# ScalarE's queue takes only the four loads of k of block 0; all loads of v of block 0 go to SyncE's queue

## The chip, the cores and the metric

The kernel runs on one core of one Trainium2 chip. The metric is the time of one execution on the device in microseconds (us). Times are medians over several executions. Each execution also has a mean granted TensorE clock, 1.00 being full speed. The clock record of a trace begins only at 5.06 in before; before that the page prints 1.00 though nothing was recorded.

Engine names in the profile: PE is TensorE (matmuls), PEld its weight loads, DVE is VectorE, ACT is ScalarE, POOL is GpSimd, SP is SyncE. ACTq and SPq are what the ScalarE and SyncE sequencers do themselves, here mostly issuing transfers (DMA).

## The reference

Attention inside chunks of 64 tokens, and then a bilinear feed-forward network (FFN) on its output:

```python
# q, k, v: (8, 8, 576, 64) float32; chunk = 64
scores = (q_c @ k_c.T) / 8;  attn = softmax(scores);  out = attn @ v_c
x = out.transpose(0, 2, 1, 3).reshape(4608, 512)
a = x @ w_a;  b = x @ w_b                  # 512 x 1536 each
return (a * b) @ w_out                     # 1536 x 512
```

## The kernel before

Tokens are worked on in nine blocks of 512. For block 0, q, k and v are loaded in small pieces, so that the first matmuls can start early; v comes in two halves (`hu`), each in four loads of 128 KB. Weights follow on SyncE's queue, first two half-width pairs, then full pairs. Two feature tiles of 128 share a pair; POOL casts each to bf16, and PE works with the cast.

```python
def load_half_v(hu, gs, eng):                       # L147
    for g in gs:
        eng.dma_start(
            out=f32[hu][2][:, g * 256:(g + 1) * 256].rearrange("p (h d) -> p h d", h=4),
            in_=v[0, 4 * hu:4 * hu + 4, g * 128:(g + 1) * 128, :].transpose([1, 0, 2]),
        )
# ... the start of the program; the order of statements is the order on each engine
for m in range(4):
    load_quads(m, 0, q, nc.sync)                    # L140
    load_quads(m, 1, k, nc.scalar)
# ... table load on ScalarE
load_half_v(0, (0, 1), nc.sync)
load_half_v(1, range(4), nc.sync)
# ...
queue_half(0, 0); queue_half(0, 1)                  # weights of pair 0: w_b, w_a, w_b, w_a (L154)
queue_w(1); queue_w(2)                              # pairs 1 and 2, w_b and w_a each

fill(2)                                             # filler matmuls that keep PE busy (L539)
quad_cast(0, 0, V)
quad_turn(0, 0, A)                                  # PE transposes q, ScalarE evacuates (L167)
load_half_v(0, (2, 3), nc.scalar)                   # <-- on ScalarE, in program order HERE
quad_cast(0, 1, V); quad_turn(0, 1, V); fill(1, n=128); quad_cast(1, 1, V)
# ... casts on POOL
quad_scores(0); expo(0, 0)                          # score products (L340), exponential on ScalarE (L245)
quad_turn(1, 0, V); quad_turn(1, 1, V); quad_turn(2, 0, A)
quad_scores(1); expo(0, 1)
# ... sums, logarithm, inverse, values of both halves; a filler; then the FFN of block 0 (L398)
```

In the trace of before the landings of transfers are counted on eight semaphores. The first eight loads wait for none of them; each of the next eighteen, on SyncE as on ScalarE, waits on one of the eight and is issued after the load last counted there has landed: the ninth, SyncE's first v load, at 4.35 us after a k load that landed at 4.33, and ScalarE's two v loads at 8.23 and 9.39 after loads that landed at 8.21 and 9.37. And later units of attention get their transposed q and k by a transpose transfer, also on SyncE's queue (L216), whose result the score products of that unit (L234) wait for.

```python
turn_unit(7); load_unit(8, (1, 2)); load_unit(9, (0,))
cast_unit(7, (2,)); some_sums(24); cast_unit(8, (0, 1))
for tg in range(4):
    step(); outs(1, (tg,))                          # four output stores, on SyncE's queue (L438)
    if tg == 0: slot(5, None)
cast_unit(8)
turn_unit(8)                                        # behind these stores in SyncE's queue (L216)
load_unit(9)
```

The softmax here doesn't subtract the row's maximum and nothing guards it: scores larger than these inputs give would overflow.

Of the kernel before, what the change touches and what calls it, by code (L numbers as in the profile page):

```python
# [11 lines left out]
def kernel(  # L12
# [10 lines left out]
    nc = tc.nc  # L23
# [118 lines left out]
            in_=src[0, 2 * m:2 * m + 2, 0:BLK, :].rearrange("h (p r) d -> p h (r d)", r=4),  # L142
        )

    def load_half_v(hu, gs, eng):
        for g in gs:
            eng.dma_start(  # L147
                out=f32[hu][2][:, g * 256:(g + 1) * 256].rearrange("p (h d) -> p h d", h=4),
                in_=v[0, 4 * hu:4 * hu + 4, g * 128:(g + 1) * 128, :].transpose([1, 0, 2]),
            )  # L150
# [152 lines left out]
    def quad_cast(m, x, eng):  # L303
        c = (m % 2) * 512
        copy(
            eng,
            qkb[m // 2][:, x, c:c + 512].rearrange("p (r h d) -> p h r d", r=4, h=2),
            f32[m // 2][x][:, c:c + 512].rearrange("p (h r d) -> p h r d", h=2, r=4),
        )

    def quad_turn(m, x, eng):

        t = nextF().bitcast(BF16)
        c0 = (m % 2) * 512
        for r in range(4):
            c = r * 128
            nc.tensor.transpose(
                t[:, c:c + 128], qkb[m // 2][:, x, c0 + c:c0 + c + 128], identity
            )
        n = 8 * x + 4 * (m % 2)  # L320
        dst = qkT[m // 2][:, n:n + 4, :]
        if x == 0:
            copy(eng, dst, t[:, 0:512].rearrange("p (r t) -> p r t", r=4))
        else:
            copy(
                eng,
                dst.rearrange("p a b -> p (a b)").rearrange("p (t r) -> p t r", r=4),
                t[:, 0:512].rearrange("p (r t) -> p t r", r=4),
            )
# [220 lines left out]
    with tc.manual_schedule():  # L550
# [6 lines left out]
        for m in range(4):  # L557
# [5 lines left out]
                name=nc.get_next_instruction_name(), act_func_set_id=6, ins=[], outs=[]  # L563
            )
        )
        load_half_v(0, (0, 1), nc.sync)
        load_half_v(1, range(4), nc.sync)

        def queue_half(i, h):
            for n, src in (("b", moe_w_b), ("a", moe_w_a)):  # L570
# [28 lines left out]
        fill(2)  # L599
        quad_cast(0, 0, V)  # L600
        quad_turn(0, 0, A)
        load_half_v(0, (2, 3), nc.scalar)
        quad_cast(0, 1, V)
        quad_turn(0, 1, V)
        fill(1, n=128)
# [288 lines left out]
```

## Time and profile before

| | before |
|---|---|
| time, 3 runs | 317.68 us median (316.77 to 318.01) |
| the profiled run | 316.13 us, span 314.3 us, mean granted clock 0.989 |
| first exponential starts | 9.87 us |
| second score products start | 10.51 us |
| first FFN matmul starts | 19.12 us |

Lines of the profile's page of the kernel before: busy time of the engines, granted clock in 40 equal slices of the span (in tenths), and shares of the chain of work that ended last.

```profile
span 314.3 us, 7288 instructions
...
PE 304.6 (97%) x2902; PEld 177.3 (56%) x2902; DVE 186.6 (59%) x371; ACT 133.9 (43%) x227; POOL 123.8 (39%) x159
...
PEclk9789999999999999999999999999999999999999
...
PE 93%; DMA 3%; ACT 2%; POOL 0%; issue 0%; DVE 0%; POOLq 0%; DVEq 0%; ACTq 0%; SPq 0%
```

PE is the limit almost everywhere; only the first slices differ. The chain before, in order of time (start, duration, what), has its transfers at the very start:

```profile
0.73 3.60 DMA f<-in_k_dram
...
4.76 4.61 DMA f<-in_v_dram
...
9.39 0.43 ACTq L147
...
9.87 0.60 ACT E L245
...
10.51 0.44 PE PS L340 x16
```

The first exponential comes after a v load and after ScalarE's issue of another one, though it needs no v. The timeline of before, ScalarE and then PE, shows it (start, duration, engine, line, operation; in brackets the idle time before it and what ended it):

```profile
5.47 0.59 ACT L167 COPY qkT<-F 128x512 bf16<-128x512 bf16 x1 [1.36 <-PE F L317]
8.23 1.59 ACTq L147 DMA_DIRECT2D f<-in_v_dram  x2
9.87 0.60 ACT L245 ACTIVATE E<-PS 128x512 bf16<-128x512 f32 x1 [3.81 <-DMA f<-in_v_dram]
...
6.44 0.42 PE L340 MATMUL PS<-qkT 64*64 64x64 bf16 x16 [0.51 <-DVE qkT L169]
...
10.51 0.42 PE L340 MATMUL PS<-qkT 64*64 64x64 bf16 x16 [2.68 <-ACT E L245]
```

The first score products are ready at 6.86 us, but ScalarE is held by its two v loads, and PE then stands until 10.51. Stretches of five microseconds of before (columns: length, busy time of PE, PEld, DVE, ACT and POOL with instruction counts, granted clock, busy share of the DMA engines, GB/s) show what follows for the clock:

```profile
5.00:10.00 5.00, 2.31 (x39) 1.75 (x38) 2.71 (x5) 0.72 (x2) 2.97 (x5) 1.00 1.16 342
10.00:15.00 5.00, 3.56 (x96) 2.64 (x96) 1.72 (x3) 4.38 (x8) 1.96 (x6) 0.69 1.18 327
15.00:20.00 5.00, 4.73 (x53) 2.03 (x45) 2.58 (x4) 2.65 (x5) 3.62 (x8) 0.63 1.09 382
20.00:25.00 5.00, 5.00 (x25) 2.29 (x24) 1.81 (x3) 1.76 (x3) 4.24 (x8) 1.00 1.09 385
```

From 11.9 to 18.7 us PE has half its clock, and the transfers run at 327 to 385 GB/s.

### The profile page before, as it was taken

Reading aid. Unit: us, or ns where it says so; the run is one execution under the profiler, and the core shown is the slowest. Engines: PE = TensorE matmul, PEld = TensorE weight load, DVE = VectorE, ACT = ScalarE, POOL = GpSimd, SP = SyncE. Lnnn points to the kernel's source line nnn. Section 1 sums busy time; section 2 is a strip of 40 time slices with the busy share of each in tenths; the row PEclk is TensorE's granted clock in tenths of the full one; section 3 lists DMA queues with packets and bytes.
Section 4 is the critical chain, followed back from the end, with each engine's and each line's share of the span. In section 5 each row is a group of like instructions: output and inputs, shape, how many; then the busy total and the mean of one; then the engine's idle time right before and its main releaser. Section 6 shows DMA issues by size and latency. Waiting matters only on the chain.

```text
span 314.3 us, 7288 instructions
## 1 busy us (share of the span) xinstructions
PE 304.6 (97%) x2902; PEld 177.3 (56%) x2902; DVE 186.6 (59%) x371; ACT 133.9 (43%) x227; POOL 123.8 (39%) x159
## 2 busy tenths in 40 slices
PE   7599999999999999999999999999999999999995
PEld 3344455874444476447644765477446744674474
DVE  3443444543447764967496749574967476646663
ACT  2643317646335542653265326442644164413320
POOL 2578869876264037402630164016500400040023
PEclk9789999999999999999999999999999999999999
DMA  7999999999999999999399249943700300020003
GB/s 262 322 383 393 380 267 244 222 272 224 204 198 254 183 219 267 185 279 208 136 257 214 68 113 216 245 100 133 136 2 0 117 22 0 3 102 31 2 0 135
DMA packets 145842, 55.00 MB, mean 175 GB/s; under 512 B 126224, under 2 KB 139792, under 8 KB 145808
## 3 DMA queue, kind: packets, MB, share of 16 engines
q1 hardware_dynamic: 143664, 53.23, 69.7%
q10 hardware_dynamic: 2144, 1.31, 1.3%
q8 instruction: 22, 0.36, 0.5%
q14 instruction: 12, 0.10, 0.1%
HBM read 37.75 MB, written 9.44 MB: 150 GB/s over the span
## 4 chain that ended last, share of the span: by engine, by line
PE 93%; DMA 3%; ACT 2%; POOL 0%; issue 0%; DVE 0%; POOLq 0%; DVEq 0%; ACTq 0%; SPq 0%
PE F L398 60%; PE F L479 19%; PE F L420 6%; PE F L251 2%; PE PS L234 2%; DMA f<-in_v_dram 1%; PE PA L267 1%; DMA f<-in_k_dram 1%; PE F L539 1%; ACT E L245 1%; PE PS L340 1%; POOL part L497 0%; ACT lns L277 0%; ACT inv L281 0%; ACT qkT L167 0%
## 5 line engine op out<-in xcount | busy, mean ns | idle before, releaser
L398 PE MATMUL F<-xT,wb 128*128 128x512 bf16 (+1 forms) x460 | 112.6, 366 | 0.0
L398 PE MATMUL F<-xT,wa 128*128 128x512 bf16 (+1 forms) x460 | 112.4, 366 | 0.0
L409 ACT CAST bsb<-F 128x512 bf16<-128x512 f32 (+1 forms) x115 | 64.1, 558 | 105.9 <-PE F L398 105.6
L410 DVE TENSOR_TENSOR ab<-F,bsb 128x512 bf16<-128x512 f32 (+1 forms) x115 | 75.2, 656 | 51.8 <-PE F L398 45.6
L398 PEld LDWEIGHTS <-wa 128*128 128x128 bf16 x460 | 45.0, 98 | 48.4
L398 PEld LDWEIGHTS <-wb 128*128 128x128 bf16 x460 | 43.6, 98 | 44.1
L497 POOL TENSOR_TENSOR part<-part 128x256 f32<-128x256 f32 x14 | 10.1, 725 | 130.0 <-ACT part L523 129.0
L169 POOL CAST qkb<-f 128x1024 bf16<-128x1024 f32 (+1 forms) x35 | 34.8, 1007 | 30.2 <-DMA f<-in_k_dram 17.4
L479 PEld LDWEIGHTS <-wst 128*128 128x128 bf16 x420 | 41.1, 98 | 4.8
L479 PE MATMUL F<-wst 128*128 128x256 bf16 x252 | 33.3, 273 | 0.0
L286 DVE TENSOR_TENSOR xT<-PA,inv 128x512 bf16<-128x512 f32 x32 | 21.8, 684 | 15.8 <-ACT inv L281 15.8
L497 DVE TENSOR_TENSOR osb<-F,part 128x256 f32<-128x256 f32 x56 | 22.3, 420 | 11.0 <-POOL part L497 8.7
L497 POOL TENSOR_TENSOR part<-part,osb 128x256 f32<-128x256 f32 x28 | 19.8, 727 | 11.4 <-DVE osb L497 11.3
L169 POOL CAST vb<-f 128x1024 bf16<-128x1024 f32 (+2 forms) x22 | 19.9, 914 | 10.1 <-DMA f<-in_v_dram 8.9
L479 PE MATMUL F<-wst,ab 128*128 128x256 bf16 x168 | 22.8, 273 | 0.0
L277 ACT ACTIVATE lns<-F 128x512 f32<-128x512 f32 x32 | 17.4, 594 | 10.7 <-PE F L251 10.7
L420 PE MATMUL F<-wo,ab 128*128 128x512 bf16 x96 | 21.9, 379 | 0.0
L467 DVE TENSOR_TENSOR wst<-ab 128x512 bf16<-128x512 bf16 x42 | 21.7, 518 | 0.0
L245 ACT ACTIVATE E<-PS 128x1024 bf16<-128x1024 f32 (+1 forms) x20 | 18.8, 941 | 6.4 <-DMA f<-in_v_dram 3.8
L468 DVE TENSOR_TENSOR wst<-ab 128x512 bf16<-128x512 bf16 x42 | 20.9, 497 | 0.0
L479 PE MATMUL F<-wo,wst 128*128 128x256 bf16 x168 | 20.6, 273 | 0.0
L497 DVE TENSOR_TENSOR part<-F,part 128x256 f32<-128x256 f32 x15 | 6.4, 425 | 21.3 <-POOL part L497 21.3
(52 smaller groups left out, 199.2 us busy)
## 6 DMA issues: line engine op xcount, KB each, us to landing
out_dram<-osb SPq DMA_DIRECT2D x31, 256.0 KB, 2.0
f<-in_q_dram SPq DMA_DIRECT2D x28, 256.0 KB, 4.2
f<-in_v_dram SPq DMA_DIRECT2D x28, 256.0 KB, 4.3
f<-in_k_dram SPq DMA_DIRECT2D x24, 256.0 KB, 4.0
wst<-in_moe_w_out_dram SPq DMA_DIRECT2D x6, 512.0 KB, 8.1
wst<-in_moe_w_b_dram SPq DMA_DIRECT2D x5, 512.0 KB, 7.7
wst<-in_moe_w_a_dram SPq DMA_DIRECT2D x5, 512.0 KB, 8.1
f<-in_v_dram SPq DMA_DIRECT2D x14, 128.0 KB, 3.3
```

The costliest lines, as they stand in the source:

```text
L169: eng.tensor_copy(out=out, in_=in_)
L245: nc.scalar.activation(out=e[:, :, s], in_=PS[:, :, s], func=AF.Exp, scale=scale)
L277: nc.scalar.activation(out=lns[:, cl, :], in_=SU[cl], func=AF.Ln)
L286: nc.vector.tensor_tensor(out=x.rearrange("p m (g c t) -> p c g m t", g=2, c=2)[:, cl], in0=PA[:, cl, :].rearrange(shape, g=2, m=4), in1=i ...
L398: nc.tensor.matmul(bank[:, 0:n], w[ft // 2][ft % 2][:, kt, :], x[:, kt, us[0] * 256:us[0] * 256 + n], start=(kt == 0), stop=(kt == NKT - 1),)
L409: nc.scalar.copy(out=bT[:, 0:n], in_=banks[0][:, 0:n])
L410: nc.vector.tensor_tensor(out=ab[ft][:, us[0] * 256:us[0] * 256 + n], in0=banks[1][:, 0:n], in1=bT[:, 0:n], op=MULT)
L420: nc.tensor.matmul(o, ab[ft][:, tg * 128:(tg + 1) * 128], wo[ft // 2][:, ft % 2, :], start=(ft == 0), stop=(ft == NFT - 1),)
L467: nc.vector.tensor_tensor(out=y[:, 0:2], in0=a[:, 0:2], in1=a[:, 2:4], op=ADD)
L468: nc.vector.tensor_tensor(out=y[:, 2:4], in0=a[:, 1:3], in1=a[:, 0:4:3], op=SUB)
L479: nc.tensor.matmul(o, a(i)[:, c:c + 128], b(i), start=(i == 0), stop=(i == NP - 1))
L497: eng.tensor_tensor(out=out, in0=in0, in1=in1, op=op)
```

## The change

The intent: ScalarE should not be held by v loads in front of its first exponential. All eight v loads of block 0 go to SyncE, ahead of the weights.

```diff
-    def load_half_v(hu, gs, eng):
-        for g in gs:
+    def load_half_v(hu, eng):
+        for g in range(4):
...
-        load_half_v(0, (0, 1), nc.sync)
-        load_half_v(1, range(4), nc.sync)
+        for hu in range(2):
+            load_half_v(hu, nc.sync)
...
         quad_turn(0, 0, A)
-        load_half_v(0, (2, 3), nc.scalar)
         quad_cast(0, 1, V)
```

The order of instructions differs only in this: ScalarE loses two issues, and SyncE gains two in front of its weight loads, between the first two v loads and the four of the other half.

## The prediction

> **What bounds the kernel now.** PE is busy 304.6 us of a 314.3 us span (97%); the chain of waits that ended last is 93% PE. In time order it is PE, with some ACT and DVE pieces, from 10.5 us on. Only its head is bound by transfers: k of block 0 until 4.33 us, the second v load (SyncE, 4.76 to 9.37), ScalarE's own issue of a v load (9.39 to 9.82), then the first exponential (9.87). So the change can move the first 20 us only.
>
> **What that head costs.** In the timeline the first score products end at 6.86 us. ScalarE then stands idle 3.81 us in front of its exponential, ended by a v transfer: its program order has two v loads there, each held until an earlier load lands (issued 8.23 and 9.39). PE waits 2.68 us for that exponential before the second score products (10.51), whose operand was ready at 8.25, when VectorE had turned k of the second pair.
>
> **What the change does.** It takes the two issues out of ScalarE's stream (1.59 us in its queue, plus the wait ahead). The exponential can start near 6.9. The next limit is VectorE's turn at 8.25, so the second score products move from 10.51 to about 8.4: 2.1 us. Carrying the later links on with traced durations (exponential 0.60, logarithm 1.02, inverse pair 1.15, turns 0.5 to 0.7), the first FFN matmul (19.12) comes about 2.1 us earlier. V lands before it is needed, so POOL no longer stands 3.04 us before its v casts (13.15).
>
> **A second effect, less sure.** By stretches, the granted clock is 1.00 until 11.9 us, 0.50 until about 18.7, then 1.00: after PE's hole from 7.83 to 10.51. [...] With the hole gone, PE probably keeps its clock. The long filler there took 2.0 us at 0.5; at full clock about 1.0, so about 1 us more. I give 60% to that.
>
> **What it adds.** Two more issues on SyncE before the weights, about 0.5 us each: the first weight load issues at about 10.0 instead of 8.95. I expect weights to land at nearly the same time, because the DMA engines are saturated there (busy share 1.1 to 1.28, 286 to 385 GB/s) and the same bytes pass. Weight casts finish at least 3.4 us before their matmuls (third feature tile: 20.0 against 23.44). Later transfers (turned unit 4 used at 64.1) have an estimated 2 to 4 us, which caps the gain near 3 us.
>
> **Sum.** 2.1 us if the clock still drops, about 3.1 if not; weighted 2.6. All of it is on the critical path: PE runs without gaps afterwards and the rest just shifts. Predicted **315.0 us**, 8 in 10 between **313.7 and 316.6**. Chances: faster by over 2% 0.02, within 2% 0.97, slower by over 2% 0.01.
>
> **What would show it right.** First exponential near 7 us, no v transfer ahead of it; PE's wait before the second score products under 0.7 us; first FFN matmul at 16 to 17 us; granted clock 1.00 through 12 to 18 us (or 0.5, with FFN at 17); first weight issue near 10 us, no PE wait on weight casts; then the same durations, chain still PE.
>
> **What would make it wrong.** Weights over 1 us later, so that POOL's casts hold the first FFN tiles; the half-clock stretch only moving, over the FFN start; a later transfer or turn with less slack, which gives the gain back before 80 us; the exponential held by something other than the v loads.

The sum: 2.1 us if the clock still drops, about 3.1 us if not, weighted 2.6. That PE keeps its clock without the hole, and the 60% on the last 1 us, are the author's estimate, from the order of events in the trace of before alone: a hole from 7.83 to 10.51 us, then half clock from 11.89 to 18.72.

## The result, and the profile after

| | before | after |
|---|---|---|
| time, 4 runs each | 317.6 us median (316.77 to 318.01) | 315.55 us median (315.03 to 315.74) |
| span of the profiled run | 314.3 us | 313.9 us |
| first exponential | 9.87 us | 7.32 us |
| second score products | 10.51 us | 8.71 us |
| first FFN matmul | 19.12 us | 16.12 us |
| first weight load issued | 8.95 us | 10.70 us |

The ratio is 0.9936 (95% interval 0.9912 to 0.996). Ratios are the mean time of one kernel's runs over that of the other's of the same rounds, so not quite the ratio of the medians quoted.

Already this table holds a riddle: the FFN starts 3.0 us earlier, the medians differ by 2.05 us, and the two profiled spans by only 0.4 us. (One part of it: the profiled run of before, 316.13 us at a clock of 0.989, is 1.5 us faster than the median of the four timed runs.) The page after:

```profile
span 313.9 us, 7288 instructions
...
PE 303.9 (97%) x2902; PEld 176.1 (56%) x2902; DVE 185.1 (59%) x371; ACT 133.8 (43%) x227; POOL 124.2 (40%) x159
...
PEclk9999999999999999999999999999999999999999
...
PE 66%; DMA 18%; SPq 8%; POOL 3%; ACT 1%; issue 1%; DVE 1%; ACTq 0%; POOLq 0%; DVEq 0%
```

The clock no longer drops in the head. But the chain, which was 93% PE, is now 66% PE and 26% transfers and SyncE's issues. The timeline after, ScalarE and PE, for the lines shown of before:

```profile
7.32 0.60 ACT L245 ACTIVATE E<-PS 128x512 bf16<-128x512 f32 x1 [1.03 <-PE PS L340]
...
6.85 0.42 PE L340 MATMUL PS<-qkT 64*64 64x64 bf16 x16 [0.51 <-DVE qkT L169]
...
8.71 0.42 PE L340 MATMUL PS<-qkT 64*64 64x64 bf16 x16
```

The exponential now waits for PE, as it should. The same stretches after, and one short stretch:

```profile
5.00:10.00 5.00, 3.94 (x67) 2.87 (x65) 2.93 (x6) 2.36 (x4) 2.45 (x4) 1.00 1.14 333
10.00:15.00 5.00, 3.28 (x90) 1.66 (x86) 2.64 (x5) 4.09 (x7) 2.57 (x6) 1.00 0.85 209
15.00:20.00 5.00, 4.73 (x48) 1.94 (x38) 1.99 (x3) 2.46 (x5) 2.69 (x6) 1.00 0.99 276
20.00:25.00 5.00, 3.91 (x18) 1.65 (x19) 1.39 (x3) 1.17 (x2) 3.67 (x7) 1.00 1.08 382
...
14.00:15.00 1.00, 1.00 (x14) 0.20 (x13) 0.04 (x1) 0.97 (x2) 0.19 (x1) 1.00 0.15 37
```

Now the transfers are the ones that starve: 209 GB/s instead of 327 from 10 to 15 us, and 37 GB/s in the microsecond from 14. The timeline of SyncE's queue after shows why, and PE's what it costs:

```profile
10.70 0.51 SPq L154 DMA_DIRECT2D wst<-in_moe_w_b_dram  x1
...
11.79 2.27 SPq L154 DMA_DIRECT2D wst<-in_moe_w_b_dram  x1
14.11 0.51 SPq L154 DMA_DIRECT2D wst<-in_moe_w_a_dram  x1
...
20.66 1.04 PE L398 MATMUL F<-xT,wb 128*128 128x512 bf16 x4 [0.69 <-POOL wb L169]
22.13 1.04 PE L398 MATMUL F<-xT,wa 128*128 128x512 bf16 x4 [0.43 <-POOL wa L169]
```

From 9.6 us SyncE issues one transfer per 0.55 us; the weights stand behind eight v loads, and one issue takes 2.27 us. The two causes are of different size: in slices of one microsecond the DMA engines are still busy at 0.97 to 1.12 from 10 to 14 us (227 to 283 GB/s), and fall to 0.15 only after the long issue. At the third feature tile PE waits for POOL's casts of late weights.

The timeline gives the start of the same PE work in each trace. Below, the lead over before (us; positive is earlier) at six points, the first three in the FFN of block 0 (its products with `w_a`) and the score products of units 2, 7 and 8. "After 2" and "after 3" are two more runs of the changed kernel from the experiments.

| trace (end of span) | tile 0 | tile 2 | tile 4 | unit 2 | unit 7 | unit 8 | end |
|---|---|---|---|---|---|---|---|
| before (314.32), start of the work | 19.56 | 23.44 | 26.89 | 48.60 | 98.44 | 108.09 | 314.32 |
| after (313.91), lead | 2.79 | 1.31 | 1.30 | 0.72 | 0.73 | 0.35 | 0.41 |
| after 2 (313.77), lead | 3.59 | 1.74 | 1.73 | 1.55 | 1.27 | 0.92 | 0.55 |
| after 3 (314.71), lead | 3.61 | 2.18 | 2.17 | 1.63 | 1.43 | -0.33 | -0.39 |

The lead of the head is won as predicted, 2.8 to 3.6 us, and then handed back in steps: at the third feature tile (weights), on the way to unit 2 (loads of unit 2; in the changed kernel's chain a k load runs from 33.46 to 44.18 us there), and at unit 8 (after 2 loses another 0.33 us at unit 9, which was not looked into). The chain in order of time near 100 us, first before:

```profile
98.91 8.74 PE F L398 x40
...
108.27 0.29 PE PS L234 x32
```

and the chain after:

```profile
98.66 2.97 DMA f<-in_q_dram
101.64 6.06 DMA qkT<-qkb
...
107.74 0.45 PE PS L234 x32
```

The same products in PE's timeline after, with the wait in brackets:

```profile
107.74 0.45 PE L234 MATMUL PS<-qkT 64*64 64x64 bf16 x32 [0.21 <-DMA qkT<-qkb]
```

Before, the transpose transfer of unit 8 was issued at 99.82 and landed 6.9 us later, at 106.7, so it had 1.4 us to spare against 108.09. SyncE's timeline before:

```profile
99.82 3.29 SPq L216 DMA_TRANSPOSE qkT<-qkb  x1
```

After, it was issued at 101.64 and landed at 107.70, 1.0 us later. What is left of the slack, 0.4 us, is all of the lead that can pass this point in this trace. The slack is not a constant: the same issue comes at 100.31 in another trace with the head of before (`before_filled`), and at 101.02 and 101.58 in the other two of the changed kernel.

### The profile page after: what moved, and what is told of

The parts are those of the page before. It is cut to its first block, busy times and chain, and to the rows that moved or that the text cites. A ratio compares the mean times of both kernels' runs of the same rounds, so it can differ in the third digit from the quotient of the medians.

```text
span 313.9 us, 7288 instructions
## 1 busy us (share of the span) xinstructions
PE 303.9 (97%) x2902; PEld 176.1 (56%) x2902; DVE 185.1 (59%) x371; ACT 133.8 (43%) x227; POOL 124.2 (40%) x159
## 3 DMA queue, kind: packets, MB, share of 16 engines
q10 hardware_dynamic: 1088, 1.05, 1.0%
## 4 chain that ended last, share of the span: by engine, by line
PE 66%; DMA 18%; SPq 8%; POOL 3%; ACT 1%; issue 1%; DVE 1%; ACTq 0%; POOLq 0%; DVEq 0%
PE F L398 42%; PE F L479 19%; DMA wst<-in_moe_w_a_dram 5%; DMA f<-in_k_dram 5%; SPq L124 5%; DMA f<-in_v_dram 4%; DMA qkT<-qkb 2%; SPq L154 2%; PE F L251 1%; POOL vb L169 1%; PE PS L234 1%; SPq L216 1%; DMA f<-in_q_dram 1%; PE PA L267 1%; PE F L420 1%
## 5 line engine op out<-in xcount | busy, mean ns | idle before, releaser
L497 POOL TENSOR_TENSOR part<-part 128x256 f32<-128x256 f32 x14 | 10.2, 725 | 126.9 <-ACT part L523 125.8
L467 DVE TENSOR_TENSOR wst<-ab 128x512 bf16<-128x512 bf16 x42 | 20.9, 497 | 0.0
L468 DVE TENSOR_TENSOR wst<-ab 128x512 bf16<-128x512 bf16 x42 | 20.9, 497 | 0.0
L245 ACT ACTIVATE E<-PS 128x1024 bf16<-128x1024 f32 (+1 forms) x20 | 18.8, 942 | 3.5 <-PE PS L234 2.5
```

The lines of the kernel that those rows point to most:

```text
L245: nc.scalar.activation(out=e[:, :, s], in_=PS[:, :, s], func=AF.Exp, scale=scale)
L467: nc.vector.tensor_tensor(out=y[:, 0:2], in0=a[:, 0:2], in1=a[:, 2:4], op=ADD)
L468: nc.vector.tensor_tensor(out=y[:, 2:4], in0=a[:, 1:3], in1=a[:, 0:4:3], op=SUB)
L497: eng.tensor_tensor(out=out, in0=in0, in1=in1, op=op)
```

## The experiments

Twelve runs were made, in three calls of four, each call on another chip (14, 12 and 10 in the record). All gave the right result. "Before" ran in the same rounds each time (11 runs a call): medians 316.36, 317.11 and 316.46 us. The changed kernel itself ran only in the first and the third call, so the edits of the second (`hold_clean`, `whole_w0`, `after_turn8`, `whole_turn8`) can be compared in their own rounds with before and with each other, but not with it. Theory, after the result: (1) ScalarE's hold was the cost in the head; (2) through PE's hole the hold also cost clock, in a varying amount; (3) the gain is handed back to transfers, because SyncE's queue runs later. Rivals: the gain comes from v landing earlier, not from the hold; the clock does not matter; the losses are accidents.

### 1. The changed kernel again: `after_again`, `after_third`

No edit.

> The changed kernel again, for its spread and for a second trace. If the late weights are part of the mechanism and no accident, the SyncE issue of the third weight load again takes about 2 us near 12 us (it took 2.27 us at 11.79), PE again waits on POOL's casts of the weights of the third feature tile (0.7 and 0.4 us), the granted clock stays at 1.00 from 5 to 40 us, and the time is 315.0 to 315.8 us, about 2 us below before. If that long issue was an accident, it is gone here and the time is about 1 us lower still.

> The changed kernel in the same rounds as the others of this call. So far 315.55 and 315.65 us, whatever the kernel before did beside it (317.6 and 316.4). Theory (the change takes the dependence on the granted clock away, and the rest of the gain is handed back to transfers): again 315.2 to 316.0; the kernel before follows its clock, about 1 us more for each 0.0054 of mean clock lost: 315.3 at 0.995, 316.2 at 0.989, 317.2 at 0.984. Rival (run to run noise unrelated to the clock): before's times do not line up with its clock.

Measured: 315.65 us (314.96 to 318.93) and 315.58 us (314.63 to 316.58), ratios 0.9983 (0.9944 to 1.0023) and 0.9965 (0.993 to 0.9999). So the changed kernel stands at 315.6, and what moves is the kernel before. Its 33 runs beside the experiments, by mean granted clock:

| mean clock of the run | runs of before | median, range (us) |
|---|---|---|
| 0.994 to 0.995 | 6 | 315.38 (315.27 to 316.36) |
| 0.989 | 8 | 316.22 (316.11 to 316.46) |
| 0.981 to 0.984 | 19 | 317.24 (316.71 to 318.33) |

Time and clock go together in before (correlation -0.91), at 0.9 us for each 0.0054 of clock. That is 1.7 us of clock in 316, or 3.4 us at half speed: half of the 6.8 us that the trace of before shows. A correlation is not yet a cause; section 3 tries the experiment. In 16 runs of the changed kernel the correlation is -0.03; their median is 315.64 us. Their clock is not always full: nine of the 16 stand at 0.993 to 0.995, as after one such stretch, and only seven at 0.998 to 1.00. In the two calls where both kernels ran side by side the medians differ by 0.71 and 0.88 us (the first ratio's interval includes 1). With the call in which only before ran the difference is 1.1 us (316.74, the median of the 33, less 315.64). It is not the 2.05 us of the first four runs, in which before stood at 317.6; against the best runs of before it is nothing, against the worst it is 1.6 us. The third trace of the changed kernel, with a clock of 1.00, ended at 314.7 us because PE waited even longer for the transpose of unit 8 (PE's timeline):

```profile
108.42 0.45 PE L234 MATMUL PS<-qkT 64*64 64x64 bf16 x32 [1.58 <-DMA qkT<-qkb]
```

The long SyncE issue came again: 1.54 us at 11.84 and 1.37 us at 11.93, and with it 0.88 and 0.33 us of PE waits (after 2). So it is no accident, but shorter than the 2.27 us of the first trace. One run of 318.93 us stays unexplained.

### 2. The hold alone: `hold_only`, `shift_only`, `hold_clean`

`hold_only` is the changed kernel with a copy on ScalarE that waits for the second v load:

```diff
+    held = buf("held", [128, 8], FP32)
...
         quad_turn(0, 0, A)
+        nc.scalar.copy(out=held, in_=f32[0][2][:, 256:264])
         quad_cast(0, 1, V)
```

> The changed kernel with the hold alone put back: ScalarE copies eight columns of the second v load before its first exponential, so it waits for that load, and issues none itself. Theory (the gain is ScalarE's hold taken away): first exponential near 10 us, second score products near 10.7, granted clock 0.5 for a stretch after about 12 us, first FFN matmul near 19 us, time 317 to 318.5, so like before. Rival (the gain comes from v landing and being cast earlier, and from less work in ScalarE's queue): first exponential may be late but the time stays within 0.7 us of the changed kernel's 315.5.

Measured: 325.65 us (324.51 to 326.76), 10 us above the changed kernel, which no theory said. The trace showed PE 6.6 us in waits for transpose transfers and transfers at 348 GB/s where the changed kernel has 382. The new buffer of 32 bytes a partition stands in front of the load buffers and moves all of them. `shift_only` keeps the buffer and drops the copy; `hold_clean` keeps the copy and writes it into the buffer of the logarithms, which exists anyway:

```diff
# shift_only, against after
+    held = buf("held", [128, 8], FP32)
# hold_clean, against after
+        nc.scalar.copy(out=lns[:, 0, 0:8], in_=f32[0][2][:, 256:264])
```

> The changed kernel with an unused buffer of 32 bytes a partition in front of the load buffers, nothing else. Theory (hold_only's extra 9 us came from the moved addresses): transfers near 350 instead of 385 GB/s at 20 to 30 us, PE waits for transposes after 60 us by several us, 322 to 326 us. Rival (hold_only was slow for its hold or its ScalarE copy): 315.6 us, no difference.

> hold_only again without its new buffer: that kernel was 10 us slower, most of it far from the start, with transfers at 350 instead of 385 GB/s, and its eight-column buffer had moved every later SBUF buffer by 32 bytes. Here ScalarE's copy goes into the buffer of the logarithms, so no address moves. Theory (the hold is what the change removed; the 10 us were the moved buffers): transfers are back at 385 GB/s at 25 to 40 us, first exponential near 10.3, first FFN matmul at 19 to 20.5 us, time 316.3 to 318.0. Rival A (the hold itself costs 10 us): about 325. Rival B (the hold does not matter at the end): 315.2 to 315.8, as the changed kernel.

`shift_only`: 325.44 us (323.38 to 326.45). The shift alone costs the 10 us. Its stretch from 20 to 25 us, to be held against that of the changed kernel above:

```profile
20.00:25.00 5.00, 4.53 (x21) 1.72 (x20) 1.95 (x3) 1.58 (x3) 2.92 (x6) 1.00 1.09 348
```

And a line of its table of waits, for PE between 20 and 130 us (waiting engine and work, what ended the wait, then the total in us, how many, and the longest):

```profile
PE PS L235 <- DMA qkT<-qkb: 6.1, 3, 3.3
```

The DMA engines are just as busy (1.09) and move 348 instead of 382 GB/s. `hold_only` thus says nothing of the hold.

`hold_clean`: 316.79 us against 317.11 for before in the same rounds, ratio 0.9982 (0.9954 to 1.0009). With the hold back, and nothing else, the kernel behaves like before: the clock of its six runs is 0.982 to 0.995, its times go with it (317.06, 317.24 and 317.56 at 0.982; 316.53 at 0.984; 315.69 at 0.989; 315.01 at 0.995). The ratio alone would not show this, since the changed kernel had 0.9983; but no run of the changed kernel has a clock under 0.993, and the two kernels without the hold in the same rounds, `whole_w0` and `after_turn8`, stand at 314.67 and 314.76 us. ScalarE's and PE's timeline:

```profile
9.40 0.20 ACT L602 COPY lns<-f 128x8 f32<-128x8 f32 x1 [3.12 <-DMA f<-in_v_dram]
9.51 0.59 ACT L245 ACTIVATE E<-PS 128x512 bf16<-128x512 f32 x1
...
10.15 0.42 PE L340 MATMUL PS<-qkT 64*64 64x64 bf16 x16 [2.01 <-ACT E L245]
```

Its first FFN products with `w_a` start at 20.31 us (before: 19.56). All eight v loads are on SyncE here, so v landing earlier is not the cause of the earlier head: the hold's removal is. The rival falls. The run is useful in another way: its transfers are issued as in the changed kernel, but no long issue falls into the stretch from 10 to 14 us, and it moves 268 GB/s from 10 to 15 us. The other two traces of the changed kernel have 265 and 264. So SyncE alone goes with the step from 327 to about 265 GB/s, and the 209 of the first trace with its longer issue, 2.27 us against 1.54 and 1.37.

### 3. The clock alone: `before_filled`

```diff
# against before
         quad_turn(2, 0, A)
+        fill(2)
         quad_scores(1)
```

> The kernel before with two filler matmul groups more in PE's hole between 7.8 and 10.5 us; ScalarE's hold stays. Theory (the clock is a second, separate part of the gain, about 1 us): first exponential still near 9.9 us, granted clock 1.00 from 5 to 20 us, first FFN matmul near 18 instead of 19.1, time about 1 us below before (316.2 to 316.9). Rival (the clock does not matter, the order of events alone does): first FFN matmul stays near 19 and the time is that of before within 0.3 us.

Measured: 316.23 us (315.46 to 316.58), ratio 0.9987 (0.9962 to 1.0012): no gain of the size expected. The stretches of its trace:

```profile
5.00:10.00 5.00, 4.13 (x43) 2.44 (x42) 2.78 (x6) 0.59 (x1) 2.62 (x5) 1.00 1.15 342
10.00:15.00 5.00, 2.99 (x96) 2.13 (x96) 1.72 (x3) 4.31 (x8) 1.44 (x4) 1.00 1.16 314
15.00:20.00 5.00, 4.50 (x43) 2.02 (x44) 2.50 (x4) 2.74 (x5) 3.72 (x8) 0.66 1.08 375
```

Filling the hole kept the clock up to 15.4 us and no further: PE is busy only 2.99 of the 5 us from 10 to 15, and the clock then falls until 18.8 us, over the fillers ahead of the FFN, whose products with `w_a` start at 19.66 instead of 19.56. So a filler in the hole moves the slow stretch rather than removes it. The clocks of its runs rose (0.992 to 1.00, against 0.983 to 0.995 of before in the same rounds), and its only run at 1.00 was its fastest, 315.46 us; but its time at 0.995 (316.4 and 316.18) is above that of before at the same clock. So the clock's share of the gain rests on the correlation in before and is not shown by the experiment made for it.

When the slow stretch comes, the kept traces show in part. In the clock records of the traces every half-clock stretch that ends before the kernel does lasts 3.41 us or twice or three times that: 14.15 to 17.57 us in `after_turn8`, 11.89 to 18.72 in before, and in `hold_clean` an estimated 10.2 us (from its mean clocks of 0.55, 0.50 and 0.93 in the three stretches of 5 us from 10 us on). The stretches at full clock are multiples too: 296.96 us in before is 87 times 3.4133, 307.20 in after 90 times. Cut each trace on that grid (`prof <label> --windows A:B`, the grid taken from its own clock record) and see how long PE was busy in the piece before:

| trace | piece (us) | PE busy, of 3.41 us | clock in the next piece |
|---|---|---|---|
| before | 8.48 to 11.89 | 1.23 | 0.50 |
| hold_clean | 7.06 to 10.47 | 1.40 | 0.50 |
| whole_w0 | 10.39 to 13.80 | 1.70 | 0.50 |
| after_turn8 | 10.74 to 14.15 | 1.70 | 0.50 |
| before_filled | 12.00 to 15.41 | 1.93 | 0.50 |
| after, after 2, after 3 | from 9.32, 9.03, 8.80 | 2.29, 2.34, 2.36 | 1.00 |

`after_turn8` has the same program as the changed kernel up to the transpose of unit 8, and the grid fell 1.4 to 1.9 us later on it. So whether the changed kernel keeps its clock seems to depend on where the grid happens to lie; its three traces were lucky. That is no rule: in the two shifted kernels of section 2, a piece near 64 us with PE busy for 1.55 and 1.77 us was followed by full clock.

### 4. The long SyncE issue: `fetch_early`

In the traces of before, of the changed kernel, of `whole_w0` and of `fetch_early` the long issue stands beside one packet of 16 KB in the queue of transfers that the profile calls instruction. A line of the table of transfer queues of the changed kernel, for 11.8 to 13.7 us:

```profile
q8 instruction: 1, 0.02, 6.0%
```

In before such a packet starts at 16.02 us, and SyncE's issue of 15.68 takes 2.58 us; in the changed kernel it starts at 11.84. There are 22 of them in a run, of 16384 bytes each, 163 to 349 PE rows (matmuls and weight loads) apart, on average 250 in before and 256 in after. In the traces of the two kernels the SyncE issue beside the first packet takes 1.4 to 2.6 us, the one ahead of it 0.51 to 0.92. It is not only the first: of SyncE's later loads of q, k and v in before (of 128 and 256 KB), the 11 that overlap such a packet take 1.46 us in the median, the other 89 take 0.82 (after: 9 with 1.72, 91 with 0.81). The test gives PE more instructions early, to see whether the packet moves and the long issue with it:

```diff
# against after
-        fill(2)
+        for _ in range(50):
+            nc.tensor.matmul(PA[0:64, 0, 0:64], ones, ones, start=True, stop=True)
         quad_cast(0, 0, V)
```

> The changed kernel with the first filler replaced by 50 tiny matmuls, 92 more PE rows in the first 5 us. Theory (SyncE's 2.27 us issue at 11.79 is a stall beside a 16 KB packet of the instruction queue[...]): that packet and the long SyncE issue come some us earlier, below 9 us, where SyncE waits for landed loads anyway; the third weight load issues in about 0.5 us, the weights of the second pair are issued by about 13 us instead of 14.7, PE's waits on POOL's casts at the third feature tile go, and the time is 0.5 to 1.5 us below the changed kernel's. Rival (the long issue belongs to SyncE's own count or to the transfer queues): it stays near 11.8 us and the time is unchanged within 0.3 us.

Measured: the packet came at 9.91 instead of 11.84 us, and the long issue with it, so the two belong together (SyncE's timeline):

```profile
10.07 1.42 SPq L154 DMA_DIRECT2D wst<-in_moe_w_b_dram  x1
11.53 0.51 SPq L154 DMA_DIRECT2D wst<-in_moe_w_a_dram  x1
```

The weights of the second pair were issued by 13.2 and 13.7 us, and PE's wait at the third tile was gone. The expected gain did not come: 316.07 us (314.49 to 319.13). The edit also changed the clock: the score products at 6.36 and 8.75 us take 0.64 us instead of 0.42, as those at 12.04 and 14.01 us of before do, where the record has 0.50; so PE probably still had half its clock there, and by the record it had it again from 13.8 to 17.2 us. So the FFN began 1.3 us later than in the changed kernel (`w_a` at 18.06), which by itself can hide that wait; and its lead of 1.5 us at unit 2 shrank to 0.35 at unit 8 and 0.36 at the end. It did not settle what the long issue costs.

### 5. What hands the gain back: `whole_w0`, `after_turn8`, `before_turn8`

`whole_w0` merges the four half loads of the first weights into two, so SyncE has ten issues ahead of the second pair, as in before (the line with `state` keeps the later staging slots where they were). `after_turn8` and `before_turn8` issue the transpose of unit 8 ahead of four output stores.

```diff
# whole_w0, against after
-        queue_half(0, 0)
-        queue_half(0, 1)
+        queue_w(0)
+        state["w"] += 2
# after_turn8 against after, before_turn8 against before
         cast_unit(8, (0, 1))
+        turn_unit(8)
         for tg in range(4):
```

> The changed kernel with the four half loads of the first weights merged into two, so SyncE has ten issues instead of twelve ahead of the second pair of weights (before: ten, too). Theory (the gain of the head is handed back because SyncE issues the weights later, one after the other at about 0.5 us each): the second pair of weights is issued about 1 us earlier than in the changed kernel, casts of it end before 20.9 us instead of 22.1, PE's waits on POOL at the third feature tile fall under 0.5 us in all, scores of unit 2 come 0.5 to 1 us earlier; the time at the end gains less, 0 to 0.5 us, if the transfers near 107 us are the last limit. Rival (weights late because of the transfer rate of v): no change of the issue to landing, waits stay near 1.1 us.

> The changed kernel with one queue position moved: the transpose transfer of unit 8 is issued ahead of four output stores instead of behind them. Theory (in the changed kernel PE, 0.7 us ahead of before at the scores of unit 7, loses half of that at the scores of unit 8, because this transpose lands too late): PE's wait for the transpose at 107.7 us is gone, scores of unit 8 about 0.3 to 0.4 us earlier, end 0.2 to 0.5 us earlier (315.0 to 315.4 on the scale of 315.6). Rival (that wait is not what sets the end): wait gone, end unchanged within 0.1 us.

> The kernel before with only the transpose of unit 8 moved ahead of four output stores. Theory (this transpose limits only a kernel whose PE comes early; in before PE did not wait there): gain of 0 to 0.5 us on average, less than the 0.8 us that the same edit gave on the changed kernel, and only in its runs with a high clock. Rival (the edit is worth the same anywhere): 0.8 us or more below before at equal clock.

| kernel | time (us) | ratio to before of its rounds | lead over before's trace at tile 2, unit 2, unit 7, unit 8, end |
|---|---|---|---|
| whole_w0 | 314.67 (314.13 to 315.81) | 0.993 (0.991 to 0.9949) | 1.84, 1.84, 1.85, 1.39, 1.42 |
| after_turn8 | 314.76 (314.45 to 316.28) | 0.9937 (0.9916 to 0.9957) | 1.67, 1.67, 1.64, 1.64, 1.57 |
| before_turn8 | 316.28 (315.58 to 317.74) | 0.9991 (0.9957 to 1.0026) | -0.05, -0.05, -0.04, -0.04, -0.15 |

In `whole_w0` the second pair of weights is issued at 11.20 and 11.75 us, not at 14.66 and 15.21 (expected: 1 us earlier), and PE's matmuls have no wait for weights at the third tile. But the merged loads of the first pair are larger (512 KB instead of 256) and land later: POOL's cast of `w_a` for the first tile ends at 17.60 us (16.71 in the trace after), and the first products with it start at 17.72. PE's load of these weights waited 0.3 us for the cast even here, behind a stretch of half clock; with PE on time the wait would probably stand at the first tile instead of the third. PE reaches tile 2 at 21.60, in the three traces of the changed kernel at 22.13, 21.70 and 21.26. Its lead at unit 2 is as large as at tile 2, where the changed kernel lost 0.2 to 0.6 us; but `after_turn8`, without this edit, loses nothing there either, so this is not shown to be the edit's doing. It loses 0.46 us at unit 8, where PE waits 0.3 us.

In `after_turn8` the lead of unit 7 passes unit 8 whole. SyncE's queue in its timeline:

```profile
98.47 2.39 SPq L216 DMA_TRANSPOSE qkT<-qkb  x1
```

The same transpose in the timeline of the changed kernel:

```profile
101.64 3.99 SPq L216 DMA_TRANSPOSE qkT<-qkb  x1
```

The transpose goes out 3.2 us earlier and PE's wait is gone. Its trace had no weight wait either, since the first FFN products came later (`w_a` at 17.89) at a half clock from about 14 to 17 us. Yet it reaches tile 2 at 21.77, about when the traces do that kept their clock: in those PE waits for the weights instead. This is a likely reason why the changed kernel's time does not follow its clock.

`before_turn8` gains nothing, at equal clock too (315.93 to 316.29 at 0.989, before 316.11 to 316.46): in before PE comes after the transpose anyway. The same queue position takes nothing off before, while in the changed kernel it removes a wait that took 0.35 to 1.76 us of the lead in three traces. At this place the change did turn a PE-bound stretch into one bound by a transfer. What the edit is worth in time against the changed kernel itself was not measured in the same rounds.

### 6. Both edits: `whole_turn8`, `whole_turn8_again`

> Both of these edits together on the changed kernel. Theory (head gain handed back at three places in turn: weights, loads of unit 2, transpose of unit 8): with the first and the last opened, more of the 3 us arrives at the end: 313.8 to 314.8 us, that is 1.5 to 2.5 us below before at the same rounds. Rival (a further transfer limit stands right behind): no better than the better of the two edits alone.

> The kernel with both follow-up edits, in the same rounds as the changed kernel: 313.9 to 314.6 us, 1.2 to 1.7 us below the changed kernel. If the difference shrinks under 0.5 us, the comparison across calls was at fault.

Measured: 314.16 us (313.9 to 315.46), ratio 0.9916 (0.9897 to 0.9935), and 314.49 us (314.16 to 316.07), ratio 0.9938 (0.9904 to 0.9971). In the rounds of the second, the changed kernel stood at 315.58; the ratio of the means is 0.9973, or 0.9 us (expected: 1.2 to 1.7), and with six runs each and a spread of 1.9 us that is not clear of noise. The lead at unit 2 (2.00 and 1.41 us in the two traces) is at the end still 2.21 and 1.58. This version beats before; that it beats the changed kernel is likely and not shown. What of the head's 3 us it still lacks is lost before tile 2: its FFN starts at 17.55 (`w_a`), not at 16. Two causes lie on each other there, a stretch of half clock from about 13 to 17 us and the merged load of `w_a`, whose cast ends at 17.32; in the second trace it ends at 18.08 and the products start at 18.13.

## Why the prediction was right or wrong

- **The hold and its length: right.** The first exponential went from 9.87 to 7.32 us (said: near 7), the second score products to 8.71 (said: about 8.4). `hold_clean` shows that the hold, not v landing earlier, is the cause.
- **The first FFN matmul: right.** 16.12 us in the first trace (said: 16 to 17); in the three traces of the changed kernel the head won 2.8 to 3.6 us.
- **The clock: right in kind, and in part luck.** In all three traces it stayed at 1.00 through the head; but nine of the 16 runs have a clock of 0.993 to 0.995, and `after_turn8`, with the same head, had half its clock from 14.15 to 17.57. The slow stretch of before lasted 6.83 us, twice 3.41, and PE was not idle in the 3.41 us ahead of it but busy for 1.23; what makes the clock drop was not shown. The prediction missed that the clock of before itself varies from run to run, so that the gain has no single size: about 0 us against the runs of before that lose one slow stretch, 1.6 us against those that lose three.
- **"I expect weights to land at nearly the same time, because the DMA engines are saturated": wrong.** A v load of 128 KB is issued every 0.55 us (0.51 us and a gap) and, at the 286 GB/s that before moves there, takes an estimated 0.46 us to move (131072 bytes / 286 GB/s), so with SyncE alone the issue is the slower of the two, and the rate falls to about 265 GB/s from 10 to 15 us. The first weight load went out at 10.70, 1.75 us later (said: 1.05 later), then came an issue of 2.27 us, and the rate fell to 37 GB/s for a microsecond. POOL's casts held the third tile: 0.69 + 0.43 us of PE waits, and the lead fell from 2.79 to 1.31 us. The other two traces show the wait again (1.2 and 0.9 us). `whole_w0` removes it at this tile but delays the first one, so it does not show what the late weights cost in all.
- **"Later transfers ... have an estimated 2 to 4 us, which caps the gain near 3 us": wrong, and this is the step that failed in the sum.** It was estimated at unit 4 alone. The transpose of unit 8 had 1.4 us in the trace of before, and in that of the changed kernel it landed 1.0 us later, so the cap was 0.4 us in the first trace (measured lead at the end 0.41) and below zero in the third. `after_turn8` and `before_turn8` show it from both sides.
- **"PE runs without gaps afterwards and the rest just shifts": wrong for the same reason.** A chain that is 93% PE says that transfers were not late in that run, not by how much they were early.
- **The total.** The time, 315.55 us, lay in the range, and 2.05 us of the 2.6 us were measured in those rounds. That closeness is luck: before stood at 317.6 there, as in its runs of low clock. In the two later calls with both kernels the gain is 0.7 to 0.9 us, over all runs 1.1 us: the mechanism of the head was right, and the share of it that reaches the end was put more than twice too high.

Open: how much the long SyncE issue and the late weights cost by themselves, how much of the gain is clock, and the run of 318.93 us.

## What to carry to other kernels

Before moving a transfer from a waiting compute engine to a queue that feeds everything, count that queue's issues, times their duration, against the data rate: here one queue with a load of 128 KB every 0.55 us feeds an estimated 238 GB/s (131072 bytes / 0.55 us), less than the 286 that two queues moved, and everything behind it comes later (the first weight load is issued at 10.70 us instead of 8.95). When the chain is all PE, look up for each later stage by how much its transfers were early; the smallest of these numbers, less what your change takes from it, is the most that an earlier PE can gain. And sort the runs of a kernel by granted clock before trusting a difference of one microsecond.
